# Where side work and block loads stand in the second half of a fused retention and feed-forward kernel

## The chip, the cores and the metric

The kernel runs on one core of a Trainium2 chip. The metric is the device time of one execution in microseconds; the median of three runs of the kernel before is 927.27 us (925.92 to 928.62). The engines have the profile's names: PE is TensorE (PEld its weight loads), DVE VectorE, ACT ScalarE, POOL GpSimd, SP SyncE. SP and ACT both issue transfers here. Each engine works through its own instructions in order, and waits on semaphores of others.

## The reference

```python
# attention: batch 8, heads 8, sequence 576, head dimension 64, fp32
scores = scale * np.matmul(q, k.transpose(0, 1, 3, 2))
gamma = 1.0 - 2.0 ** (-5.0 - np.arange(H, dtype=np.float32))
rel = pos[:, None] - pos[None, :]
Dmat = np.where(rel >= 0, gamma[:, None, None] ** rel[None, :, :], 0.0)
out = np.matmul(scores * Dmat[None], v)
# (B, H, S, D) -> x of (4608, 512), then the feed-forward part; the weights are float64
a = x @ w1            # 512 x 1024
b = x @ w2
h = a * b @ w3        # 1024 x 1024
return (h @ w_out).astype(np.float32)   # 1024 x 512
```

## The kernel before, in words

**Attention in rounds.** The decay is split into a factor for q and one for k and v, so that the retention runs in chunks with a carried state. Batches go in pairs; the sequence is cut into NC = 5 chunks, one of 64 rows and four of 128. There are G = 20 rounds `g`, four pairs by five chunks. A round transposes q and k of the next chunk (`front`, `front_blocks`), scales q and v (`scale_blocks` L184, `scale`, on GpSimd), and multiplies scores (L232), state (L254) and output (L273, L298).

**Loads by blocks.** `load_blocks` (L159) brings q or k of a chunk in pieces of 32 by 32, so that VectorE's block transpose (L189) finishes the transposition. That takes 16 transfers for a full chunk and 8 for the short one, of 32 KB each in runs of 128 bytes; all are issued by SyncE (L170). From round 7 on both q and k come so (`in_blocks`). The tiles of both share a pool tag with two buffers, so that the blocks of a round can come only when those of the round before have been transposed.

**The feed-forward part** multiplies by a form of Strassen's algorithm with seven products. `w3 @ w_out` is multiplied out beforehand. `up` (L506) is one step with one level, for the first tokens. For the later ones `up2` (L959) is one step of a second level: seven products of two matmuls, in PSUM tiles of a pool with seven buffers, of which ScalarE copies the first (L991) and VectorE adds the others (`plus`, L980), each addition on the result of the one before; ScalarE copies the first tile a second time (L1003), GpSimd combines steps (`combine`, L985), VectorE multiplies the two halves (`multiply`, L948). What comes last in a step, the product that goes on in p5's tile and its addition, is left to the next step (`rest`, `finish`). A group has 14 such steps, and then three `down` (L623), each of seven products of four matmuls and their sums and stores.

**The forms of the weights** for the second level are computed once by VectorE (`weight_forms`, L841), stored in HBM (`kept`) and read back, 896 KB a step, into a ring of three (`next_forms`, L899). `open_second` (L883) starts this: it issues the first two loads.

**The order of the work** is written out by hand. The list `todo` holds the items (`up`, `up2`, `down`); `dealt` says how many a round does (1, 1, 2, 2, 2, 3, 4, 4, 4, 3, 7, 7, 3, 7, 7 for rounds 5 to 19), and `work(n)` does n of them. The list `aside` holds side operations: transposes of the next round, and the sums that a `down` needs ahead (`ahead`). In `up2` one is taken after each `plus` (L982), in `down` all that are left ahead of the last addition (L680). `spread` does the same with VectorE's operations on the weights. In the loop of rounds (L1063 to L1118) a round with blocks first scales q of the next chunk (L1076), does all items but one, puts the two transposes into `aside`, does the last item, and then loads the blocks of q and k of the chunk after that.

The program runs through its items in the order written; a transfer also waits for an earlier one that used the same completion semaphore, and the two issuing queues share these.

Of the kernel before, what the change touches and what calls it, by code (L numbers as in the profile page):

```python
# [19 lines left out]
def kernel(  # L20
# [13 lines left out]
    nc = tc.nc  # L34
# [7 lines left out]
    BL = 32  # L42
# [5 lines left out]
    NC = (S + P - 1) // P  # L48
# [107 lines left out]
        live["S", fp] = True  # L156
        yield

    def load_blocks(g, nm):  # L159

        i, c = divmod(g, NC)
        n = sizes[c] // BL
        t = pools["ld"].tile([P, 2 * NP, P // BL, BL], F32, tag="ld_q", name="bl_" + nm)
        src = {"k": k, "q": q}[nm][2 * i:2 * i + 2].rearrange("b (p a) s d -> a (b p) s d", a=2)
        for a in range(2):
            for f in range(D // BL):
                part = (a * (D // BL) + f) * BL
                for m in range(n):
                    s0 = starts[c] + m * BL
                    nc.sync.dma_start(t[part:part + BL, :, m, :],  # L170
                                      src[a, :, s0:s0 + BL, f * BL:(f + 1) * BL].rearrange("m r x -> r m x"))
        live["bl_" + nm, g] = t

    def scale_blocks(g):
# [387 lines left out]


    aside, owed, spread = [], [], []

    def w3_sums():

# [55 lines left out]
    def down(x, y, then=None, last=False):  # L623
        a, done, left = pair_of(x, y)
        ahead(x, y)
        while len(done) < 3:
            aside.pop(0)()
        if then:
            ahead(*then)
        ps = {}  # L630
        ot = pools["ot"].tile([P, 2, 2, DM // 2], F32, tag="ot", name="ot")

        def product(nm, A, B, on=None):
            ps[nm] = ps[on] if on else acc.tile([P, DM // 2], F32, tag="acc", name="po")
            for f in range(NP):
                nc.tensor.matmul(ps[nm], a[A][:, f, :], live["W"][B][:, f, :], start=(f == 0 and not on),  # L636
                                 stop=(f == NP - 1), skip_group_check=True)

        def plus(nm, to, sb):
            nc.vector.tensor_add(ot[:, to[0], to[1]], ps[nm], ot[:, sb[0], sb[1]])  # L640
            if spread:
                spread.pop(0)()

        def put(m, t, row, half=slice(0, 2)):

            i, n = every[m]
            r0 = t * P
            while r0 < (t + 1) * P:
                b = r0 // TB
                e = min((b + 1) * TB, (t + 1) * P)  # L650
                r = (2 * i + b) * S + n * TB + r0 - b * TB
                stores.append((out[r:r + e - r0, half.start * DM // 2:half.stop * DM // 2],
                               ot[r0 - t * P:e - t * P, row, half].rearrange("p h d -> p (h d)")))
                r0 = e
            if not keep_stores:
                store()

        C11, C12, C21, C22 = (0, 0), (0, 1), (1, 0), (1, 1)
        product(1, "A11", "B11")
        first = ot[:, 0, 0]  # L660
        if "first" in live:
            first = live["first"].pop(0)
            live["first"].append(first)
        nc.scalar.copy(first, ps[1])  # L664
        product(7, "S3", "T3")
        product(2, "A12", "B21", on=1)
        nc.vector.tensor_tensor(out=a["S4"], in0=a["A12"], in1=a["S2"], op=ALU.subtract)
        product(6, "S2", "T2")
        nc.vector.tensor_add(ot[:, 0, 1], ps[6], first)
        nc.scalar.copy(ot[:, 0, 0], ps[2])  # L670
        plus(7, C21, C12)
        product(5, "S1", "T1")
        plus(5, C22, C21)
        product(4, "A22", "-T4")
        plus(4, C21, C21)
        put(*y, 1)
        if last:
            put(*x, 0, slice(0, 1))
        product(3, "S4", "B22", on=5)
        while aside:  # L680
            aside.pop(0)()
        plus(3, C12, C12)
        put(*x, 0, slice(1 if last else 0, 2))

    stores, keep_stores = [], []
# [197 lines left out]
    def open_second():  # L883
        while spread:
            spread.pop(0)()
        ra = [wp.tile([P, 32 * P], F32, tag=f"wA{h}", name="ra") for h in halves]
        cs = [wp.tile([P, 2, 4, 2, TB], F32, tag=f"wS{h}", name="cc") for h in halves]
        ring.extend([ra[0][:, :FORM], ra[0][:, FORM:2 * FORM], ra[1][:, :FORM]])
        free.extend(cs[h][:, j] for h in halves for j in range(2))
        live["first"] = [ra[0][:, 2 * FORM + j * DM // 2:2 * FORM + (j + 1) * DM // 2] for j in range(2)]  # L890
        live["T2"] = ra[1][:, FORM:].rearrange("p (s k c t) -> p s k c t", s=2, k=3, c=2)
        live["E"] = ffn.tile([P, 4, 2, TB], F32, tag="c", name="e", bufs=1).rearrange("p (e r) b t -> p e r b t", e=2)
        live["E4"] = pools["carry"].tile([P, KF, P], F32, tag="carry", name="e4").rearrange("p f n -> p (f n)")[
            :, :4 * TB].rearrange("p (r b t) -> p r b t", r=2, b=2)
        for _ in range(2):
            next_forms()
        live["U"] = [ffn.tile([P, 2, TB], F32, tag="T", name="u", bufs=5) for _ in range(5)]

    def next_forms():  # L899
        n = sent[0]  # L900
        if n < 14 * len(groups):
            nm = NAMES.index(OPERANDS[order[n % 7]][0])
            nc.scalar.dma_start(ring[n % 3], kept[n % 14 // 7][nm])
            sent[0] += 1

    def token_forms(gr):
# [52 lines left out]
    def up2(gr, n):  # L959
# [19 lines left out]

        def plus(ps, to, sb):  # L980
            nc.vector.tensor_add(c[:, to], ps, c[:, sb])  # L981
            if aside:  # L982
                aside.pop(0)()

        def combine(part):  # L985
            for into, of in adds:
                o, i = sums2[into][:, part], sums2[of][:, part]
                nc.gpsimd.tensor_tensor(out=o, in0=o, in1=i, op=ALU.add)  # L988
# [3 lines left out]
        p6 = product(None, "S2", "T2")  # L992
        finish()
        next_forms()
        plus(p6, 1, 0)
        plus(product(None, "S3", "T3"), 2, 1)
        p5 = product(None, "S1", "T1")
        plus(p5, 3, 2)
        plus(product(None, "A22", "-T4"), 2, 2)
        combine(slice(2, 4))  # L1000
        multiply()
        product(p1, "A12", "B21")
        nc.scalar.copy(c[:, 0], p1)  # L1003

        def rest():
            product(p5, "S4", "B22")
# [46 lines left out]
    g = NC  # L1053
# [9 lines left out]
    for g in range(NC, G):  # L1063
        c = g % NC
        n = dealt[g - NC]
        if g + 2 < G and not in_blocks[g + 2]:
            load(g + 2, "k")
            load_blocks(g + 2, "q")
        if g + 1 < G:
            scale(g + 1, "v")  # L1070
            if not in_blocks[g + 1]:
                front(g + 1, "k")
                front_blocks(g + 1, "q")
        half = (n + 1) // 2
        if in_blocks[g + 1]:
            scale_blocks(g + 1)  # L1076

            work(n - 1)
            aside.extend(lambda nm=nm: front_blocks(g + 1, nm) for nm in "kq")
            work(1)  # L1080
            while aside:
                aside.pop(0)()
            half = 0
        elif g + 1 == G:
            work(n)
            half = 0
        if in_blocks[g + 2]:
            load_blocks(g + 2, "q")
            load_blocks(g + 2, "k")
        work(half)  # L1090
        pv(g)()

        if g + 2 < G:
            queue = nc.scalar if in_blocks[g + 2] else nc.sync
            load(g + 2, "v", queue)
            if in_blocks[g + 2] and (g + 2) % NC != NC - 1:
                load(g + 2, "k")
        if g + 1 < G:
# [65 lines left out]
```

## Time and profile before

| | |
|---|---|
| time, median of three | 927.27 us |
| span of the profiled run | 920.9 us |
| mean granted clock of TensorE | 0.962 |
| PE, PEld busy | 90%, 81% |
| DVE, POOL, ACT busy | 67%, 41%, 24% |
| moved by transfers | 128.78 MB, 140 GB/s on average |

The chain of work that ended last is by engine: PE 52%, DVE 19%, DMA 12%, SyncE's issuing 7%. In a line of the waits the columns are: who waited, for whom, how long in total, how often, and the longest. In a line of the timeline: start, duration, engine, line, operation, what it writes from what it reads, how many merged, and in brackets how long the engine stood idle before and who released it. Rounds of the second level lie about so in time: round 10 ends near 409 us, 11 near 439, 12 near 476, 13 near 513, 14 near 557, 15 near 596, 16 near 647, 17 near 689, 18 near 729, 19 near 775; then come three `down`, the last 14 steps and the last three `down`.

### The profile page before, as it was taken

How to read it: one execution, taken by the hardware profiler on the slowest of the kernel's cores; microseconds unless marked ns; L12 is line 12 of the kernel's file. 1: busy time of each engine (PE TensorE's matmuls, PEld its weight loads, DVE VectorE, ACT ScalarE, POOL GpSimd, SP SyncE). 2: the span in 40 equal slices, each digit the busy share in tenths (PEclk: the TensorE clock that was granted, in tenths of full speed). 3: DMA queues.
4: the chain of work that ended last, by engine and by line, in shares of the span. 5: the costliest groups of instructions: out<-in, count | busy, mean ns of one | idle time of the engine just before them, and what ended most of it. 6: DMA issues, size and time to landing. Idle time of an engine off the chain costs nothing.

```text
span 920.9 us, 15659 instructions
## 1 busy us (share of the span) xinstructions
PE 831.1 (90%) x6049; PEld 744.5 (81%) x6049; DVE 613.1 (67%) x931; ACT 224.1 (24%) x429; POOL 376.8 (41%) x251
## 2 busy tenths in 40 slices
PE   7999999999999789588696999987999998899988
PEld 6889999447899767488685879977889997798977
DVE  4989999945444776156577745868646878568753
ACT  4786565820211000111111002211011220011200
POOL 1100010011031210566638934858915779537730
PEclk7999999999999999789897999998999999999999
DMA  9994643551364775987585208875428451154401
GB/s 190 219 211 105 117 123 114 154 88 16 74 130 87 193 206 184 243 187 206 138 199 151 46 37 226 224 196 149 88 61 216 160 200 50 37 183 167 154 24 46
DMA packets 247402, 128.78 MB, mean 140 GB/s; under 512 B 202904, under 2 KB 229272, under 8 KB 247328
## 3 DMA queue, kind: packets, MB, share of 16 engines
q1 hardware_dynamic: 203296, 54.86, 29.9%
q10 hardware_dynamic: 44032, 72.92, 24.7%
q8 instruction: 47, 0.77, 0.4%
q14 instruction: 27, 0.22, 0.1%
HBM read 105.46 MB, written 22.28 MB: 139 GB/s over the span
## 4 chain that ended last, share of the span: by engine, by line
PE 52%; DVE 19%; DMA 12%; SPq 7%; issue 5%; POOL 4%; ACT 1%; ACTq 0%; DVEq 0%; POOLq 0%
PE po L636 17%; PE up L976 16%; PE up L523 7%; PE ps L476 6%; SPq L170 5%; DVE cc L981 4%; DVE ab L956 4%; DMA bl_q<-in_q_dram 4%; DMA bl_k<-in_k_dram 3%; DMA kept<-wA 2%; POOL cc L988 2%; PE xps L298 2%; DMA ld_v<-in_v_dram 2%; PE sc L232 2%; DVE c L528 1%
## 5 line engine op out<-in xcount | busy, mean ns | idle before, releaser
L988 POOL TENSOR_TENSOR cc<-cc 128x768 f32<-128x768 f32 x112 | 208.8, 1884 | 86.7 <-DVE cc L981 85.2
L981 DVE TENSOR_TENSOR cc<-up,cc 128x384 f32<-128x384 f32 x280 | 151.3, 552 | 60.4 <-PE up L976 41.6
L636 PE MATMUL po<-w3o,ab 128*128 128x256 f32 x552 | 129.3, 389 | 24.1 <-ACT ra L664 18.6
L636 PEld LDWEIGHTS po<-w3o,ab 128*128 128x128 f32 x552 | 105.8, 194 | 42.4 <-ACT ra L664 20.2
L976 PE MATMUL up<-xT,ra 128*128 128x192 f32 x512 | 107.3, 341 | 31.1 <-DVE cc L981 18.4
L976 PEld LDWEIGHTS up<-xT,ra 128*128 128x128 f32 x512 | 88.2, 196 | 36.6 <-DVE cc L981 22.1
L203 POOL TENSOR_TENSOR ld_v<-ld_v,gk 128x1024 f32<-128x1024 f32 (+1 forms) x18 | 34.4, 1911 | 174.1 <-DMA ld_v<-in_v_dram 172.1
L956 DVE TENSOR_TENSOR ab<-cc 128x384 f32<-128x384 f32 x64 | 82.8, 1334 | 32.7 <-POOL cc L988 32.7
L180 POOL TENSOR_TENSOR bl_q<-bl_q,gqs 128x512 f32<-128x512 f32 (+1 forms) x30 | 30.5, 1038 | 119.1 <-DMA bl_q<-in_q_dram 93.9
L976 PE MATMUL up<-ra 128*128 128x192 f32 x384 | 77.8, 333 | 0.7 <-DMA ra<-kept 0.6
L1003 ACT COPY cc<-up 128x384 f32<-128x384 f32 x56 | 26.8, 479 | 206.1 <-PE up L976 138.2
L976 PE MATMUL up<-e,ra 128*128 128x192 f32 x384 | 73.4, 327 | 1.1 <-DVE cc L981 0.9
L523 PE MATMUL up<-xT,wA 128*128 128x192 f32 x384 | 70.7, 328 | 0.3 <-DVE xT L495 0.3
L528 DVE TENSOR_TENSOR c<-up,c 128x384 f32<-128x384 f32 x80 | 44.0, 549 | 36.6 <-PE up L523 36.0
L976 PEld LDWEIGHTS up<-ra 128*128 128x128 f32 x384 | 66.0, 194 | 1.5 <-PE up L976 1.2
L636 PE MATMUL po<-wB,forms 128*128 128x256 f32 x288 | 65.3, 380 | 2.0 <-DVE forms L609 2.0
L976 PEld LDWEIGHTS up<-e,ra 128*128 128x128 f32 x384 | 64.3, 191 | 1.7 <-DVE cc L981 1.2
L523 PEld LDWEIGHTS up<-xT,wA 128*128 128x128 f32 x384 | 63.3, 190 | 1.7 <-PE up L523 0.6
L636 PEld LDWEIGHTS po<-wB,forms 128*128 128x128 f32 x288 | 54.6, 190 | 10.1 <-issue 1.9
L976 PE MATMUL up<-u,ra 128*128 128x192 f32 x288 | 56.3, 333 | 5.7 <-DVE cc L981 5.7
L235 DVE TENSOR_TENSOR pm<-sc,mask 128x512 f32<-128x512 f32 (+1 forms) x80 | 45.4, 626 | 23.4 <-PE sc L232 23.4
L640 DVE TENSOR_TENSOR ot<-po,ot 128x256 f32<-128x256 f32 x72 | 30.4, 422 | 38.4 <-PE po L636 37.6
(106 smaller groups left out, 1235.4 us busy)
## 6 DMA issues: line engine op xcount, KB each, us to landing
ra<-kept ACTq DMA_DIRECT2D x56, 896.0 KB, 4.7
raw<-in_moe_w_dram SPq DMA_DIRECT2D x72, 128.0 KB, 3.0
bl_q<-in_q_dram SPq DMA_DIRECT2D x216, 32.0 KB, 3.2
ld_k<-in_k_dram SPq DMA_DIRECT2D x13, 512.0 KB, 6.0
bl_k<-in_k_dram SPq DMA_DIRECT2D x192, 32.0 KB, 2.4
kept<-wA SPq DMA_DIRECT2D x24, 256.0 KB, 3.3
out_dram<-ot ACTq DMA_DIRECT2D x23, 256.0 KB, 2.0
ld_v<-in_v_dram ACTq DMA_DIRECT2D x11, 512.0 KB, 5.7
```

Source lines behind the costliest of these rows:

```text
L170: nc.sync.dma_start(t[part:part + BL, :, m, :], src[a, :, s0:s0 + BL, f * BL:(f + 1) * BL].rearrange("m r x -> r m x"))
L180: nc.gpsimd.tensor_tensor(out=part, in0=part, in1=gqs[:, :, n0:n0 + n].unsqueeze(3).to_broadcast([P, NP, n, BL]), op=ALU.mult)
L203: engine.tensor_tensor(out=t, in0=t, in1=gam[:sz, c].unsqueeze(1).unsqueeze(3).to_broadcast([sz, 2, H, D]), op=ALU.mult)
L235: nc.vector.tensor_mul(pm[:sz, b, j, :, :sz], sc[j][:sz, :, :sz], mask[:sz, :sz].unsqueeze(1).to_broadcast([sz, NP, sz]))
L476: nc.tensor.matmul(ps, live["w3T", ft][:, g, :], live["wo"][:, g, :], start=(g == 0), stop=(g == KF - 1))
L523: nc.tensor.matmul(ps[:, w, :], a[:, w, r, :], b[:, r, :], start=(new and w == r == 0), stop=(w == r == 1), skip_group_check=True)
L528: nc.vector.tensor_add(c[:, to], ps, c[:, sb])
L636: nc.tensor.matmul(ps[nm], a[A][:, f, :], live["W"][B][:, f, :], start=(f == 0 and not on), stop=(f == NP - 1), skip_group_check=True)
L956: nc.vector.tensor_mul(ab, v[:, :, 0, :], v[:, :, 1, :])
L976: nc.tensor.matmul(ps[:, w, :], weight_of(slot, a, w), B[b], start=(new and w == 0), stop=True, skip_group_check=True)
L981: nc.vector.tensor_add(c[:, to], ps, c[:, sb])
L988: nc.gpsimd.tensor_tensor(out=o, in0=o, in1=i, op=ALU.add)
```

## The change

Five edits, which all move work and take none away:

1. q of the next chunk is scaled ahead of the last two items of a round and not ahead of all. It is meant to keep GpSimd from waiting for blocks with the combinations queued behind.
2. From round 10 on the blocks of k are put in a list `small`, which ScalarE issues: four after the first form load of a step and four after its second copy, or at two places of a `down`; what is left goes ahead of the scaling.
3. An `up2` step takes one side operation, after its four first additions, in place of one after each addition.
4. From round 10 on a `down` takes a side operation after each addition but the last, and what is left after the last addition in place of ahead of it.
5. The first two form loads are issued by SyncE, and the second sums of the weights start one slot of `spread` later.

```diff
+    small = []
+
+    def issue(n):
+        for _ in range(min(n, len(small))):
+            small.pop(0)()
+
-    def load_blocks(g, nm):
+    def load_blocks(g, nm, later=False):
...
-                    nc.sync.dma_start(t[part:part + BL, :, m, :],
-                                      src[a, :, s0:s0 + BL, f * BL:(f + 1) * BL].rearrange("m r x -> r m x"))
+                    to = t[part:part + BL, :, m, :]
+                    of = src[a, :, s0:s0 + BL, f * BL:(f + 1) * BL].rearrange("m r x -> r m x")
+                    if later:
+                        small.append(lambda to=to, of=of: nc.scalar.dma_start(to, of))
+                    else:
+                        nc.sync.dma_start(to, of)
...
# in down
             nc.vector.tensor_add(ot[:, to[0], to[1]], ps[nm], ot[:, sb[0], sb[1]])
             if spread:
                 spread.pop(0)()
+            if g >= 2 * NC and aside and nm != 3:
+                aside.pop(0)()
...
         nc.scalar.copy(first, ps[1])
+        issue(4)
         product(7, "S3", "T3")
...
         nc.scalar.copy(ot[:, 0, 0], ps[2])
+        issue(4)
         plus(7, C21, C12)
...
         product(3, "S4", "B22", on=5)
+        while aside and g < 2 * NC:
+            aside.pop(0)()
+        plus(3, C12, C12)
         while aside:
             aside.pop(0)()
-        plus(3, C12, C12)
...
# in open_second
         for _ in range(2):
-            next_forms()
+            next_forms(nc.sync)
...
# in up2
         def plus(ps, to, sb):
             nc.vector.tensor_add(c[:, to], ps, c[:, sb])
-            if aside:
-                aside.pop(0)()
...
         finish()
         next_forms()
+        issue(4)
...
         combine(slice(2, 4))
+        if aside:
+            aside.pop(0)()
         multiply()
         product(p1, "A12", "B21")
         nc.scalar.copy(c[:, 0], p1)
+        issue(4)
...
# in the loop of rounds
         if in_blocks[g + 1]:
+            work(n - 2)
+            issue(len(small))
             scale_blocks(g + 1)
-
-            work(n - 1)
             aside.extend(lambda nm=nm: front_blocks(g + 1, nm) for nm in "kq")
-            work(1)
+            work(2)
             while aside:
                 aside.pop(0)()
...
             load_blocks(g + 2, "q")
-            load_blocks(g + 2, "k")
+            load_blocks(g + 2, "k", later=g >= 2 * NC)
...
-            forms = [(lambda h=h, second=second: spread.extend([lambda: None] * second + weight_forms(h, second)),)
+            forms = [(lambda h=h, second=second: spread.extend([lambda: None] * (2 * second) + weight_forms(h, second)),)
                      for h in halves for second in (False, True)]
```

More of the change, by code (lines that the diff above doesn't have):

```diff
@@ L564 @@
     aside, owed, spread = [], [], []
+    g = 0
     def w3_sums():
@@ L895, in open_second, with next_forms @@
         for _ in range(2):
-            next_forms()
+            next_forms(nc.sync)
         live["U"] = [ffn.tile([P, 2, TB], F32, tag="T", name="u", bufs=5) for _ in range(5)]
-    def next_forms():
+    def next_forms(engine=nc.scalar):
         n = sent[0]
@@ L902, in next_forms @@
             nm = NAMES.index(OPERANDS[order[n % 7]][0])
-            nc.scalar.dma_start(ring[n % 3], kept[n % 14 // 7][nm])
+            engine.dma_start(ring[n % 3], kept[n % 14 // 7][nm])
             sent[0] += 1
```

## The prediction

> **What bounds the kernel now.** I read the page's shares and slices first, then the table by stretches, then the waits, then the timeline round each stretch in which TensorE stands still.
>
> ```profile
> PE 831.1 (90%) x6049; PEld 744.5 (81%) x6049; DVE 613.1 (67%) x931; ACT 224.1 (24%) x429; POOL 376.8 (41%) x251
> PEclk7999999999999999789897999998999999999999
> 440.00:475.00 35.00, 24.66 (x219) 23.36 (x219) 21.71 (x30) 5.39 (x11) 17.38 (x11) 0.90 0.67 165
> 475.00:510.00 35.00, 25.97 (x188) 24.28 (x188) 23.68 (x32) 3.83 (x8) 23.66 (x14) 0.81 0.59 147
> 600.00:640.00 40.00, 30.89 (x186) 29.48 (x188) 28.79 (x43) 5.26 (x12) 27.88 (x16) 0.91 0.63 178
> ```
>
> The columns of the last three are busy PE, PEld, DVE, ACT, POOL, then clock, DMA share and GB/s. TensorE is the bound on the whole, but between 300 and 690 us it loses up to ten of 35 us to idle time, and its granted clock falls to 0.81. Nothing else is full there: those stretches wait in chains.
>
> ```profile
> POOL bl_q L180 <- DMA bl_q<-in_q_dram: 93.9, 3, 80.5
> POOL bl_q L180 <- DMA bl_k<-in_k_dram: 21.9, 5, 5.4
> DVE ab L956 <- POOL cc L988: 32.7, 11, 8.5
> ACT xT L305 <- DMA kept<-wA: 21.0, 1, 21.0
> SPq L170 <- DMA ra<-kept: 31.1, 13, 6.6
> ```
>
> GpSimd waits in L180 for the blocks of q, and VectorE's multiplications (L956) wait for GpSimd's combinations (L988), which are queued behind it. Round 12 shows the chain whole:
>
> ```profile
> 445.17 16.51 SPq L170 DMA_DIRECT2D bl_k<-in_k_dram  x16
> 449.74 2.06 POOL L180 TENSOR_TENSOR bl_q<-bl_q,gqs 128x512 f32<-128x512 f32 x2 [5.40 <-DMA bl_k<-in_k_dram]
> 453.60 4.22 DVE L956 TENSOR_TENSOR ab<-cc 128x384 f32<-128x384 f32 x2 [8.51 <-POOL cc L988]
> 455.89 2.93 PE L976 MATMUL up<-xT,ra 128*128 128x192 f32 x8 [7.70 <-ACT cc L991]
> ```
>
> The other kinds of hole are VectorE's transposes and sums between two additions (504.75, 637.40), the same ahead of the last addition of a down (531.48), and ScalarE caught in the first form loads (380.68):
>
> ```profile
> 371.41 4.48 ACTq L903 DMA_DIRECT2D ra<-kept  x2
> 380.68 3.49 PE L636 MATMUL po<-w3o,ab 128*128 128x256 f32 x8 [11.19 <-ACT ra L664]
> 504.75 1.65 PE L976 MATMUL up<-xT,ra 128*128 128x192 f32 x4 [5.09 <-DVE cc L981]
> 531.48 1.99 PE L636 MATMUL po<-w3o,ab 128*128 128x256 f32 x8 [2.69 <-ACT ra L664]
> 637.40 1.65 PE L976 MATMUL up<-xT,ra 128*128 128x192 f32 x4 [4.72 <-DVE cc L981]
> L170 SPq DMA_DIRECT2D bl_q<-in_q_dram x216: 311/449/2487, 193.2 to 695.7; - x108
> ```
>
> **What the Trainium skill says.** "TensorE: Matmul & The Clock Gate", section "What's actually happening", has the clock halved after about 3.4 us of idleness. The trace agrees: after the holes of 5.09 and 4.72 us four records take 1.65 us, otherwise 0.81. A long hole so costs some 2.7 us more. "DMA: Bandwidth & Descriptors", section "Issuing engines are not separate DMA queues", says that a second issuing engine saves only issue time, as all transfers share 16 engines. Here an issue is 0.449 us on SyncE's queue, and 16 blocks take 8 to 16.5 us. "SBUF — State Buffer", section "SBUF: two separate sides", has VectorE and GpSimd lock one port pair against each other. The trace agrees: the sum of L605 takes 0.68 us alone and up to 2.24 us beside GpSimd.
>
> **The change, part by part.** A second-level step has 28 matmul records, four per 0.65 us: 4.55 us. State, values and scores add 1.03 + 1.90 + 0.93 + 1.99 = 5.85 us to a round (433.70 to 439.5). The floor of a round is 24.05 us with four steps and 37.7 us with seven.
>
> 1. *Scaling ahead of the last two items, k off SyncE's queue, transposes one per step.* Rounds 11, 12, 13 and 16 took 30.5 (409.0 to 439.5), 36.8 (to 476.3), 36.75 (to 513.05) and 50.8 us (596.05 to 646.87): 6.4 + 12.7 + 12.7 + 13.1 = 44.9 us over their floors, holes and cold clock together. Rounds 15 and 18 (38.1 and 40.2 us) have nothing much to give. With the scaling two steps later q's blocks have had about 15 us to land (12 us of issue and 3 us of flight) and GpSimd no longer stands in front of the combinations. VectorE does per step five additions of 0.55 us and 8/7 multiplications of 1.33 us: 4.27 us. With 2.5 us of transposes and 2.5 us of masking that is 22.1 of 24.05 us in a four-step round, so little slack is left, and I don't count on the floor: 75%, 34 us. Bounds: half (22 us), 90% (40 us).
>
> 2. *k's 16 blocks on ScalarE, in fours.* No row shows block issues on this queue. From below: 0.449 us each with 0.04 between, 7.9 us per round of 16. From above: about 1 us each, SyncE's slowest round (16.5 us for 16). Eight go into each of two steps, on top of two copies of 0.48 us and a form load of 0.33 us. Laid out over the 4.55 us step: the form load goes at 2.0 us, as it waits for the ring, the first four issues end by 4.3 us (cheap) or 5.2 us (one slowed by the form load ahead of it), the copy of L1003 follows, four more end at 7.0 to 7.7 us, and only then does the next step's first copy (L991) run, which was ready at 5.2 us. In the second step the delay grows to between 2.5 and 4 us. Queued behind it are L1003, which frees a PSUM bank that the third product of the next step takes, L991, on which all of VectorE's additions of that step hang, and the next form load, which has about 2.4 us to spare (4.7 us to land). With cheap issues all just fits, 0.5 us; with dear ones TensorE waits some 5 us. I take 2.3 us in each of the six rounds with steps (11, 12, 13, 15, 16, 18): 14 us; bounds 3 and 30. The waits between transfers raise the upper end: blocks on SyncE already waited 31.1 us for form loads to land, so a block on ScalarE may wait likewise, with the copies behind it.
>
> 3. *The flush of what is left ahead of the scaling.* In round 17 only one down precedes it, so eight issues, about 4 us, stand ahead of L664 of the second down. That copy releases the bank of the third product, 3.5 us after the down's start. I take 2.5 us (0 to 5).
>
> 4. *Side operations in a down.* After the last addition, and spread over the earlier ones, the sums no longer hold back the store and the copy that TensorE waits for: 2.69 + 1.63 + 3.05 (at 788.36) = 7.4 us. Against it, in round 14 the transpose of q now sits in the second down, at about 534 us, while GpSimd has q scaled only at 538 us, behind the token sums. I take 5 us (3 to 7).
>
> 5. *First forms by SyncE.* ScalarE's copy comes some 5 to 9 us sooner and most of the hole at 380 us closes. But the next stage hangs on SyncE: blocks of q from 373.31 us, of k from 386.23 to 394.5 us, transposed at 400.11 us, and scores at 405.26 us. The two loads now stand ahead of these blocks and wait for the stores of the weights, and the transpose of k moves one step forward. TensorE, early, then waits for k. The gain is given back: I take a loss of 1 us (gain 3 to loss 4). The extra empty slot in `spread` moves VectorE's weight sums past one addition, away from a wait for stores (the hole of 4.01 us at 321 us), and sends the last forms about 2 us later; it ends in the same wait, at nothing.
>
> Sum: 34 + 5 - 14 - 2.5 - 1 = 21.5 us; 927.3 - 21.5 = **906 us**.
>
> **The rivals.**
> - *Everything fits* (cheap issues, 90% of the excess, all three holes of the downs, flush and forms free): 40 + 7 - 3 = 44 us, **883 us**. For it: ScalarE is busy 24%, and two steps have room for 10.5 us of its work in 9.1 us, nearly enough. Against it: VectorE's thin slack and round 17.
> - *The transfers are the bound anyway*: k by another queue lands no sooner, as the DMA engines are 0.6 to 0.75 busy in these stretches, and the transpose, one step earlier, waits. Only 35% of the excess comes back: 16 + 5 - 14 - 2.5 - 1 = 3.5 us, **924 us**. For it: SyncE takes up to 16.5 us for 16 blocks, far above 16 times 0.449. Against it: q and k went one after the other before and now overlap.
> - *ScalarE becomes the bound*, and the kernel slower: 60% of the excess and 4 us of the downs (31 us), against 30 us of stalls, 5 of flush and 4 of forms: 8 us slower, **935 us**. For it: every addition of a step hangs on a copy of this queue, which issues and waits in order. Against it: it idles most of a step today.
>
> **How the numbers follow.** The forecast has 0.57, everything fits 0.15, transfers 0.12, ScalarE 0.16. Predicted is the forecast's 906 us. The range runs from 886 us, near the best case, to 930 us, past the transfers' case; outside lie most of the slower case and the tail of the best. Faster by over 0.3% (under 924.5 us): 0.57 + 0.15 + 0.07 of the transfers' case = 0.79; within 0.3%: 0.05; slower: 0.16.
>
> **What would show it.** Right: the waits of L180 for blocks shrink to a few us in rounds 11 to 13 and 16, no hole of TensorE there is above 3 us, and the clock stays above 0.95; L956 waits under 15 us for GpSimd; the holes at the downs are gone. ScalarE's copies L991 and L1003 start late in the first two steps of a round, with short holes of TensorE behind them. The hole at 380 us is smaller and one ahead of the scores near 400 us is larger. Wrong: form loads that TensorE waits for, or a ScalarE queue standing on another transfer for over 5 us, would mean the slower case; a transpose of k that waits for its blocks for several us in each round, the transfers' case.

## The result and the profile after

The changed kernel takes **937.72 us** (median of three, 936.82 to 942.21) against 927.27: a ratio of 1.0128 with the 95% interval [1.0085, 1.0171]. Run again on another chip it came to 1.0069 [1.0034, 1.0105]. It is slower by 6 to 12 us. The forecast was 906 us, range 886 to 930, with 0.16 for slower.

The engines' busy time, and TensorE's busy tenths and granted clock over 40 slices, of the kernel after (its profiled run is the one of 942.21 us, with a span of 939.5 us and a mean clock of 0.953; a slice is 23.5 us):

```profile
PE 843.4 (90%) x6049; PEld 754.1 (80%) x6049; DVE 613.6 (65%) x931; ACT 224.1 (24%) x429; POOL 378.9 (40%) x251
PE   8899999999995997758797999978899998999988
PEclk7999999999997998989998999898999999999999
```

The work of VectorE, ScalarE and GpSimd is the same to within about 2 us. TensorE is busy 12.3 us longer with as many instructions, that is at a lower clock, and idle 6.3 us longer. Its row has a 5 in the 13th slice (282 to 305 us), and the clock a 7, where the kernel before has nines (its slice from 276 to 299 us); later the clock stays below nine tenths in five slices between 352 and 658 us, as many as before.

Two of the stretches that the prediction showed, in the kernel after (columns as there: busy PE, PEld, DVE, ACT, POOL, then clock, DMA share, GB/s):

```profile
440.00:475.00 35.00, 27.84 (x247) 26.66 (x246) 25.20 (x35) 6.44 (x13) 23.80 (x15) 0.90 0.87 196
600.00:640.00 40.00, 33.65 (x235) 32.23 (x232) 26.25 (x43) 6.40 (x14) 22.53 (x14) 0.92 0.67 173
```

TensorE does get more done in them (27.84 and 33.65 us busy against 24.66 and 30.89; 31.01 against 25.97 in the third, 475 to 510 us). So the edit works where it was aimed. The waits say the same, and show what came in its place (who waited, for whom, total, times, longest):

```profile
DVE kT L199 <- DMA bl_k<-in_k_dram: 23.4, 2, 11.8
PE up L993 <- ACT cc L1006: 20.7, 14, 5.1
ACT cc L1006 <- DMA bl_k<-in_k_dram: 20.1, 5, 5.9
PE up L533 <- DVE c L538: 14.3, 4, 10.6
ACT ra L677 <- DMA bl_k<-in_k_dram: 13.3, 1, 13.3
DVE ab L973 <- POOL cc L1003: 12.2, 8, 3.0
```

GpSimd's scaling (L190, before L180) waits 2.6 us for blocks of the round in place of 21.9, and VectorE's multiplications (L973, before L956) wait 12.2 us for GpSimd in place of 32.7. In their place there are three new waits: ScalarE's copies in the steps (L1006, before L991) and in a `down` (L677, before L664) stand behind block issues, and VectorE stands at a transpose of k for 11.8 us, which becomes 10.6 us of TensorE in the first-level step `up` (L533).

**Where the time went.** I cut both traces at the ends of the scores of each round, worked out from the timelines (us; the differences are of the unrounded times):

| rounds | before | after | after - before |
|---|---|---|---|
| 7 | 25.5 | 37.7 | +12.2 |
| 8, 9, 10 | 110.2 | 113.4 | +3.2 |
| 11, 12, 13, 14 | 148.4 | 137.4 | -10.9 |
| 15, 16, 17, 18 | 171.8 | 184.1 | +12.3 |

Round 19, the last steps and the last `down`s add nothing (-0.1 us); about 2 us of the spans' difference lie ahead of all this, in the start. A table like this compares one execution with one other: the spans differ by 18.6 us, the medians by 10.4, and a second trace of the changed kernel (after_again below) has 36.8, 112.3, 134.7 and 182.0 us in these four rows. So differences of 2 to 3 us in a row say little, while those of 10 us and more stand. One round that the prediction doesn't mention loses more than rounds 11 to 14 gain.

Round 7 in the kernel before, in the timeline (start, duration, engine, line, operation, and the idle time before with its releaser):

```profile
288.11 1.25 DVE L189 STREAM_TRANSPOSE kT<-bl_k 128x1024 f32<-128x1024 f32 x1 [2.22 <-DMA bl_k<-in_k_dram]
291.44 1.57 PE L523 MATMUL up<-xT,wS 128*128 128x192 f32 x8 [1.02 <-DVE c L528]
```

and in the kernel after:

```profile
290.52 1.25 DVE L199 STREAM_TRANSPOSE kT<-bl_k 128x1024 f32<-128x1024 f32 x1 [11.79 <-DMA bl_k<-in_k_dram]
293.85 2.93 PE L533 MATMUL up<-xT,wS 128*128 128x192 f32 x8 [10.59 <-DVE c L538]
```

The blocks of k land at about the same point of the round in both, some 15 us after the scores of the round before (273.3 and 275.3 us). Round 7 has two items. Before, the transposes came in the second of them, so VectorE had the additions of the first to do and waited 2.22 us. Now `work(n - 2)` does nothing there, the transposes sit behind the first additions of the first `up`, and VectorE stands still for 11.79 us with all later additions behind it; TensorE runs out of PSUM tiles and comes back cold (2.93 us for eight matmuls, warm 1.57).

Rounds 12, 16 and 17 of the kernel after show the second new wait (ACTq is ScalarE's queue issuing transfers):

```profile
462.72 5.29 ACTq L179 DMA_DIRECT2D bl_k<-in_k_dram  x4
468.11 0.48 ACT L1006 COPY cc<-up 128x384 f32<-128x384 f32 x1 [4.94 <-DMA bl_k<-in_k_dram]
468.64 2.93 PE L993 MATMUL up<-xT,ra 128*128 128x192 f32 x8 [5.08 <-ACT cc L1006]
...
608.64 0.33 ACTq L920 DMA_DIRECT2D ra<-kept  x1
...
616.16 1.83 ACTq L179 DMA_DIRECT2D bl_k<-in_k_dram  x4
618.03 0.48 ACT L1006 COPY cc<-up 128x384 f32<-128x384 f32 x1 [5.91 <-DMA bl_k<-in_k_dram]
618.56 0.92 PE L993 MATMUL up<-xT,ra 128*128 128x192 f32 x4 [3.46 <-ACT cc L1006]
...
677.75 0.37 ACT L677 COPY ra<-po 128x256 f32<-128x256 f32 x1 [13.27 <-DMA bl_k<-in_k_dram]
678.17 3.65 PE L647 MATMUL po<-w3o,ab 128*128 128x256 f32 x8 [3.89 <-ACT ra L677]
```

Four issues take 1.83 us when they follow each other, and 5.29 us when one of them has to stand. What it stands for can be read in the trace: the issue waits on its own completion semaphore, which an earlier form load used. In round 12 the load issued at 459.66 us lands at 467.67 us, and the last of the four blocks goes at 467.69 us. In round 16 the load of 608.64 us lands at 616.14 us, and the queue, free since 612.1 us, stands for 4.0 us ahead of the first of its four blocks, at 616.16 us. Over the whole trace ScalarE's queue stands 19.8 us for form loads, its own ones. The copy that opens the next step follows the last issue within 0.1 us, and TensorE follows the copy: it waits 5.08 us in round 12 and 3.46 us in round 16. In round 17 it is the flush, and there no issue stands: eight in a row take 4.00 us, with the copy of the second `down` behind them, for which TensorE waits 3.89 us. (The 13.27 us in front of that copy are idle time of ScalarE's arithmetic, not of its queue.)

### The profile page after: what moved, and what is told of

The parts are those of the page before. It is cut to its first block, busy times and chain, and to the rows that moved or that the text cites. A ratio compares the mean times of both kernels' runs of the same rounds, so it can differ in the third digit from the quotient of the medians.

```text
span 939.5 us, 15664 instructions
## 1 busy us (share of the span) xinstructions
PE 843.4 (90%) x6049; PEld 754.1 (80%) x6049; DVE 613.6 (65%) x931; ACT 224.1 (24%) x429; POOL 378.9 (40%) x251
## 4 chain that ended last, share of the span: by engine, by line
PE 55%; DVE 17%; DMA 12%; POOL 4%; issue 4%; SPq 4%; ACT 2%; ACTq 1%; POOLq 0%; DVEq 0%
PE po L647 19%; PE up L993 13%; PE up L533 11%; DVE ab L973 6%; PE ps L486 6%; DVE cc L998 5%; DMA ra<-kept 4%; PE sc L242 2%; PE xps L308 2%; DMA ld_v<-in_v_dram 2%; POOL cc L1003 2%; SPq L181 2%; DMA bl_k<-in_k_dram 2%; DMA bl_q<-in_q_dram 1%; ACTq L179 1%
## 5 line engine op out<-in xcount | busy, mean ns | idle before, releaser
L998 DVE TENSOR_TENSOR cc<-up,cc 128x384 f32<-128x384 f32 x280 | 152.1, 555 | 79.4 <-PE up L993 36.4
L647 PEld LDWEIGHTS po<-w3o,ab 128*128 128x128 f32 x552 | 105.6, 194 | 29.8 <-ACT ra L677 10.1
L973 DVE TENSOR_TENSOR ab<-cc 128x384 f32<-128x384 f32 x64 | 88.9, 1430 | 12.3 <-POOL cc L1003 12.2
L647 PE MATMUL po<-wB,forms 128*128 128x256 f32 x288 | 69.6, 398 | 6.8 <-DVE forms L620 6.8
L533 PE MATMUL up<-xT,wA 128*128 128x192 f32 x384 | 72.1, 333 | 0.0
L538 DVE TENSOR_TENSOR c<-up,c 128x384 f32<-128x384 f32 x80 | 44.1, 551 | 42.1 <-PE up L533 41.5
L993 PEld LDWEIGHTS up<-ra 128*128 128x128 f32 x384 | 64.1, 190 | 9.1 <-ACT cc L1006 9.0
L647 PEld LDWEIGHTS po<-wB,forms 128*128 128x128 f32 x288 | 57.7, 201 | 16.5 <-DVE forms L620 4.0
L190 POOL TENSOR_TENSOR bl_q<-bl_q,gqs 128x512 f32<-128x512 f32 (+1 forms) x30 | 31.0, 1054 | 92.3 <-DMA bl_q<-in_q_dram 89.7
L533 PEld LDWEIGHTS up<-xT,wA 128*128 128x128 f32 x384 | 65.1, 194 | 1.1 <-issue 0.5
L681 DVE TENSOR_TENSOR ab<-ab,forms 128x512 f32<-128x512 f32 x17 | 17.9, 1056 | 58.2 <-PE po L647 58.2
L486 PE MATMUL ps<-wo,w3T 128*128 128x512 f32 x128 | 55.1, 592 | 0.0
```

The source lines that it names most:

```text
L190: nc.gpsimd.tensor_tensor(out=part, in0=part, in1=gqs[:, :, n0:n0 + n].unsqueeze(3).to_broadcast([P, NP, n, BL]), op=ALU.mult)
L486: nc.tensor.matmul(ps, live["w3T", ft][:, g, :], live["wo"][:, g, :], start=(g == 0), stop=(g == KF - 1))
L533: nc.tensor.matmul(ps[:, w, :], a[:, w, r, :], b[:, r, :], start=(new and w == r == 0), stop=(w == r == 1), skip_group_check=True)
L973: nc.vector.tensor_mul(ab, v[:, :, 0, :], v[:, :, 1, :])
L993: nc.tensor.matmul(ps[:, w, :], weight_of(slot, a, w), B[b], start=(new and w == 0), stop=True, skip_group_check=True)
```

## The experiments

My theory after this: (a) round 7 alone costs 11 to 12 us and has nothing to do with the aim of the change; (b) ScalarE's issues cost some 14 us, as forecast; (c) the scaling later in the round is a gain, but below the 34 us forecast. The rivals: the loss is all ScalarE's; or the early order is a loss everywhere and round 7 only its largest part; or the first forms by SyncE upset rounds 9 and 10. The twelve kernels were run in three groups. A ratio is to the kernel before, on the same chip, whose medians were 928.10, 928.81 and 931.68 us. All kernels start from the changed one.

**late10: the order of before up to round 10, all else as changed.** First group, with the next three.

```diff
+            early = g > 2 * NC
+            if early:
-            work(n - 2)
-            issue(len(small))
+                work(n - 2)
+                issue(len(small))
             scale_blocks(g + 1)
+            if not early:
+                work(n - 1)
+                issue(len(small))
             aside.extend(lambda nm=nm: front_blocks(g + 1, nm) for nm in "kq")
-            work(2)
+            work(2 if early else 1)
```

> The changed kernel, but up to round 10 with the order of before: scaling ahead of all items, all items but one, then both transposes in the last item. Theory A (the transposes, moved one item forward, meet blocks of k that SyncE has not yet brought: hole of 10.6 us in round 7, of 8.5 us in round 10): some 12 us come back, about 925 us, near the kernel before. Theory B (ScalarE's issuing of blocks costs the time): at most 3 us come back, 934 us or more.

Measured: 923.44 us, 0.994 [0.9909, 0.9971]. Against the changed kernel's 1.0069 to 1.0128 this gives back 1.3 to 1.9% of 928 us, 12 to 17 us. Round 7 takes 25.0 us again.

```profile
286.78 1.25 DVE L199 STREAM_TRANSPOSE kT<-bl_k 128x1024 f32<-128x1024 f32 x1 [1.69 <-DMA bl_k<-in_k_dram]
```

This line of late10 stands for the one with 11.79 us above: the blocks land as before, VectorE waits 1.69 us, and TensorE afterwards 0.49 us. Theory (a) holds. The other rounds that this run puts back, 8 to 10, take 114.0 us against 113.4, so the time comes from round 7.

**ksync: all blocks of k by SyncE, all else as changed.**

```diff
-            load_blocks(g + 2, "k", later=g >= 2 * NC)
+            load_blocks(g + 2, "k")
```

> The changed kernel, but all blocks of k issued by SyncE, none by ScalarE. Theory A: nothing comes back, 937 to 945 us, as the gain of rounds 11 to 13 shrinks. Theory B: the holes of TensorE behind ScalarE's copies go (20.7 us of waits in the trace), 922 to 928 us.

Measured: 921.55 us, 0.9899 [0.9852, 0.9947]. Round 7 stays long (36.4 us), while rounds 15 to 18 fall from 184.1 to 168.2 us. Against the changed kernel's ratios this gives back 16 to 21 us.

**late10_ksync: both.**

> Both of the first two together: order of before up to round 10, and all blocks of k by SyncE. Theory A alone: as the first of these, about 925 us or a few us above. Theory B alone: as the second, 922 to 928 us. Both hold and add: 910 to 918 us, faster than the kernel before.

Measured: 911.67 us, 0.9788 [0.9742, 0.9834]. Against late10 the step is 1.5% of 928 us, 14 us, by the medians 11.8; against ksync it is 10 us. The waits of this kernel, beside those of after:

```profile
DVE kT L199 <- DMA bl_k<-in_k_dram: 22.5, 5, 7.7
PE up L993 <- ACT cc L1006: 5.3, 6, 2.9
```

TensorE's wait for ScalarE's copies falls from 20.7 us (17.2 in late10) to 5.3. VectorE still waits little for GpSimd (10.1 us), so this gain did not need k on another queue. What ScalarE's issues did buy is seen best in round 11 of late10_ksync:

```profile
434.65 1.25 DVE L199 STREAM_TRANSPOSE kT<-bl_k 128x1024 f32<-128x1024 f32 x1 [6.95 <-DMA bl_k<-in_k_dram]
436.39 1.19 PE L283 MATMUL xps<-qT,sb 64*64 64x128 f32 x28 [4.23 <-DVE cc L998]
```

With SyncE bringing both, k comes late and TensorE loses 4.23 us (round 11: 30.5 us against 27.8 in late10). In round 13 k's transpose waits once more, 4.02 us; VectorE's multiplication and ScalarE's next copy stand behind it, and TensorE waits 2.88 us, which is part of the 5.3 us above. So two of the suspects add up: the order up to round 10 and ScalarE's issues together are worth more than the whole loss, and the rest of the change is a gain of 2.1% (16 us by the medians, 20 by the ratio).

**fscal: the first two form loads by ScalarE again.**

```diff
-            next_forms(nc.sync)
+            next_forms()
```

> The changed kernel, but the first two form loads issued by ScalarE as before. Theories A and B: within 4 us of the changed kernel, 934 to 942 us. Theory C (the loads ahead of the blocks on SyncE's queue delay rounds 9 and 10): 6 us or more come back, 931 us or less.

Measured: 930.55 us, 1.0028 [0.9999, 1.0056], 4 to 9 us below the changed kernel. The blocks behind the first form loads (which SyncE issues at 386.84 us), in the kernel after:

```profile
388.29 15.03 SPq L181 DMA_DIRECT2D bl_q<-in_q_dram  x16
388.37 3.49 PE L647 MATMUL po<-w3o,ab 128*128 128x256 f32 x8 [5.17 <-ACT ra L677]
403.42 12.64 SPq L181 DMA_DIRECT2D bl_k<-in_k_dram  x16
419.69 1.76 PE L308 MATMUL xps<-pm,ld_v 64*64 64x64 f32 x28 [8.46 <-DVE cc L998]
```

and in fscal:

```profile
380.82 13.07 SPq L181 DMA_DIRECT2D bl_q<-in_q_dram  x16
388.32 3.78 PE L647 MATMUL po<-w3o,ab 128*128 128x256 f32 x8 [11.30 <-ACT ra L677]
393.99 9.11 SPq L181 DMA_DIRECT2D bl_k<-in_k_dram  x16
410.68 1.03 PE L308 MATMUL xps<-pm,ld_v 64*64 64x64 f32 x28 [2.83 <-DVE cc L998]
```

With the loads on ScalarE the hole at 380 us is whole (11.30 us) and the later one small (2.83); with SyncE they are 5.17 and 8.46. The sums are 14.1 and 13.6 us: the hole is moved. Round 10 is all the same 3.9 us longer with the loads on SyncE (47.8 us against 43.9). On SyncE the blocks wait behind the two loads and are also slower to issue (27.7 us for 32, against 22.2).

**l10_ks_fs: late10_ksync and fscal in one.** Second group, with the next three.

> The kernel with the order of before up to round 10 and all blocks of k by SyncE, and the first two form loads by ScalarE again. Theory C (the loads ahead of the blocks on SyncE's queue delay round 10, which took 49.8 us with them and 44.9 us before): some 5 us come back, about 907 us. Rival (the delay has another cause): within 2 us of the version without this edit, 911 us.

Measured: 911.73 us, 0.9832 [0.9782, 0.9881]. That is not below late10_ksync's 0.9788, so the forms by SyncE cost something measurable only beside ScalarE's issues, if at all. The intervals overlap, and are too wide to show or exclude the 5 us of theory C here.

**l10_ks_fs_s1: the same with the weight sums at the old place of `spread`.**

```diff
-            ... spread.extend([lambda: None] * (2 * second) + weight_forms(h, second)) ...
+            ... spread.extend([lambda: None] * second + weight_forms(h, second)) ...
```

> The same, and the second sums of the weights one slot of the spread list earlier, as before. Rounds 8 and 9 together take 65.3 us before and 64.4 us in the version with the order of before up to round 10, so the slot is expected to be worth nothing: within 2 us of the kernel without this edit. Rival (the later slot sends the last forms late and costs round 9 what it gives to round 8): 3 us or more faster.

Measured: 910.73 us, 0.9817 [0.9779, 0.9855], no difference that the intervals could show. Round 8 goes from 24.4 to 29.7 us and round 9 from 41.4 to 34.6: the slot moves the waits from one round into the other (TensorE's longest one is 3.65 us in round 8 with the early slot, 9.40 us in round 9 with the late one).

**no_down: l10_ks_fs with `down` as before the change.**

```diff
-            if g >= 2 * NC and aside and nm != 3:
-                aside.pop(0)()
...
-        while aside and g < 2 * NC:
-            aside.pop(0)()
-        plus(3, C12, C12)
         while aside:
             aside.pop(0)()
+        plus(3, C12, C12)
```

> The order of before up to round 10, k by SyncE, first forms by ScalarE, and the downs as before, with all side operations ahead of the last addition. The prediction's 5 us for the edit in the downs: some 5 us slower than with that edit, holes of 2 to 3 us at the downs back. Rival (the edit is worth nothing, as in the rounds after 19 the changed kernel gained nothing): within 2 us.

Measured: 912.15 us, 0.9837 [0.9794, 0.988], against 911.73: no gain of the edit of `down` is seen. Each interval is about 4 us wide to either side, so the run does not exclude the 5 us either. The traces show a part given back: no_down has holes of 1.83, 1.82 and 1.92 us (rounds 14, 17 and after 19) ahead of the matmuls that wait for a copy, which l10_ks_fs lacks, while the holes ahead of the first matmuls of a `down`, which wait for a sum of VectorE (L616), add up to 5.7 us in rounds 14 and 17 of l10_ks_fs and to 2.6 in no_down.

A second loss at the `down`s is in both of these kernels, so it does not explain their equal times, but it explains why the last part of the kernel after gains nothing. The hole of 3.05 us of before at 788.36 us is gone there, but the first `down` of each last three now starts late. The last such start of the kernel after:

```profile
902.99 5.41 PE L647 MATMUL po<-wB,forms 128*128 128x256 f32 x16 [3.56 <-DVE forms L620]
```

where before has

```profile
886.04 3.72 PE L636 MATMUL po<-wB,forms 128*128 128x256 f32 x16 [0.46 <-DVE forms L609]
```

(The other pair is 3.26 us, then 5.38, against 1.50 and 3.69.) The sums that a `down` needs are side operations of the last step ahead of it. Edit 3 moves them from behind the first addition to behind the fourth, next to the multiplications, so they come 2 to 3 us later, and the 16 matmuls run at a lower clock, for a further 1.7 us.

**l10_twos: late10 with `issue(2)` in all four places.** Half the dose, to see whether the loss goes with the number of issues in front of a copy or with the queue as such.

> The order of before up to round 10, ScalarE issuing the blocks of k, but two and not four at each place. If ScalarE loses by more issue time than two steps hold, half the dose over twice the steps fits: rounds 16 and 18 come down from 51 and 40 us to about 46 and 39, 916 us or less. If it loses by waits on earlier transfers, whatever the dose, the time stays at 920 to 925 us.

Measured: 917.92 us, 0.9902 [0.9866, 0.9937], between late10 (0.994) and late10_ksync (0.9788). TensorE's wait for L1006 falls from 17.2 to 9.1 us, and rounds 16 and 18 reach 44.1 and 38.9 us, all that k by SyncE gives there. The time lies between the two expectations, and the dose is not cleanly halved: what the steps no longer take falls to the flush. In rounds 11 to 13 ten blocks go in one row (4.8 to 6.4 us), and in round 17 twelve:

```profile
651.47 6.00 ACTq L179 DMA_DIRECT2D bl_k<-in_k_dram  x12
657.93 3.78 PE L647 MATMUL po<-w3o,ab 128*128 128x256 f32 x8 [5.88 <-ACT ra L677]
```

Twelve issues stand before the copy, TensorE waits 5.88 us where after has 3.89, and round 17 takes 51.5 us against 48.1 in late10 (round 14: 47.4 against 43.8). With twos the queue also stands less for form loads (5.3 us in all, 14.4 in late10), so this run does not tell the two causes apart.

**l10_twos_d4: twos in the steps, fours in a `down`.** Third group, with the last three.

> The order of before up to round 10, ScalarE issuing the blocks of k, two at each place of a step and four at each place of a down. With twos everywhere round 17 took 51.5 us, as twelve blocks were left to flush. If ScalarE's loss is issue time in front of copies, round 17 comes back to 48 us and rounds 16 and 18 stay at 44 to 46 and 39 us: 912 to 916 us. If not, 918 us or more.

Measured: 916.28 us, 0.9855 [0.9815, 0.9896], between the two expectations again. The flush in round 17 is eight issues again and its hole 3.88 us, as in after. But the rounds hardly follow: 50.4 us for round 17, and 47.0 for round 14, where the flush's hole is gone and one ahead of the first matmuls of the `down`, which waits for a sum of VectorE (L616), grew from 1.71 to 3.28 us. I can't say where the other 2 us of round 17 went; its trace is of the execution of 921.51 us, and the median is 916.28.

**after_again: the changed kernel once more**, to have it on the chip of the others.

> The changed kernel itself, beside the versions made from it and on the same chip: 1.01 to 1.015 of the kernel before, as measured first.

Measured: 937.17 us, 1.0069 [1.0034, 1.0105], a little less than expected; the interval reaches 1.01.

**late9: as late10, but the order of before only up to round 9.** It asks whether the hole of 8.46 us in round 10 comes from the early transposes as well.

```diff
-            early = g > 2 * NC
+            early = g > 2 * NC - 1
```

> The order of before only up to round 9; round 10 as in the changed kernel. If the hole of 8.5 us in round 10 comes from the transposes one item early, it stays here and goes in the version with the order of before up to round 10: some 5 us slower than that one, 928 us. If it comes from the first form loads on SyncE's queue, both are alike, 921 to 925 us, and round 7 alone explains what the order of before brings.

Measured: 925.21 us, 0.9942 [0.9922, 0.9962], the same as late10. Its hole in round 10 is 8.91 us, ahead of the product with v (L308); late10 has one of 9.36 us just behind that, ahead of the state (L264), which ends in a wait for the load of k's rows. The hole is there with either order, and small with the forms on ScalarE (fscal 2.83 us, best 2.89). So it belongs to edit 5. Of the rounds whose order both kernels undo, only round 7 gets shorter by it (8 to 10 together: 113.4 in after, 114.0 in late10). The rival that the early order loses everywhere falls with this, and with rounds 11 to 13, which keep it in late10_ksync and are 12 us below before; the rival that ScalarE loses everything fell with late10, which leaves ScalarE's issues as they are.

**best: late9 and k by SyncE and forms by ScalarE, and the first sum of a `down` behind the first addition of the last step.** The sum goes into a list of its own, `soon`:

```diff
         def plus(ps, to, sb):
             nc.vector.tensor_add(c[:, to], ps, c[:, sb])
+            if soon:
+                soon.pop(0)()
...
-            ahead(*nxt[1:], 1 if fn is up2 else 3)
+            ahead(*nxt[1:], 1 if fn is up2 else 3, soon if fn is up2 else None)
```

> What the runs point to: order of before up to round 9, all blocks of k by SyncE, first forms by ScalarE, side operations one per step from round 10 on, but the first sum of the next down after the first addition of the last step, as before. Theory (the end of each group loses as this sum waits behind the multiplications; tail of 114 us against 111.5): 2 us better than the other versions without ScalarE's issuing, 908 us or less. Rival (the sum's place is worth nothing): 910 to 913 us.

Measured: **909.79 us, 0.9776 [0.9745, 0.9808]**, faster than both kernels, but above the 908 us of the theory and just below the rival's 910. The starts of the last `down`s are those of before again, here the last:

```profile
874.79 3.72 PE L647 MATMUL po<-wB,forms 128*128 128x256 f32 x16 [0.45 <-DVE forms L620]
```

The three `down`s after round 19 take 38.3 us in place of 41.6 before, and the last three 42.0 in place of 47.2 in late10_ksync (before 42.3). In the ratios that is 0.56 points to l10_ks_fs (5 us) and 0.12 to late10_ksync (1 us); the intervals overlap, so the worth of the sum's place is not shown. The kernel still has round 11's hole for k's blocks (4.72 us).

Rounds in groups, for the kernels that the argument uses (us, from the timelines):

| rounds | before | after | late10 | ksync | late10_ksync | best |
|---|---|---|---|---|---|---|
| 7 | 25.5 | 37.7 | 25.0 | 36.4 | 25.3 | 26.3 |
| 8 to 10 | 110.2 | 113.4 | 114.0 | 112.8 | 114.5 | 112.0 |
| 11 to 14 | 148.4 | 137.4 | 135.2 | 136.7 | 136.2 | 136.2 |
| 15 to 18 | 171.8 | 184.1 | 181.6 | 168.2 | 170.3 | 171.6 |

## Why the prediction was wrong

The sum failed in its first term: step 1 took the cost of the new order outside the rounds it was aimed at as nothing, without a reason, and so left out round 7; and it counted too much gain. The total of the costs of ScalarE's issues and of the flush was sized well. Between 906 us and what was measured lie 28 to 32 us: some 12 are round 7, and some 18 a gain of steps 1, 4 and 5 of 20 us in place of 38. Gains have a plus here, losses a minus.

1. **Scaling ahead of the last two items (forecast: +34 us). This step failed, in two ways.** It counted the excess of rounds 11 to 13 and 16 and took for granted that the new order costs nothing elsewhere. But the loop runs from the first round with blocks on, and in round 7, with two items, it puts the transposes ahead of blocks that land 15 us into the round. This lost 12.2 us in the trace and 12 to 17 us in the ratios of late10. The information was in the trace of before: VectorE's transpose of round 7 already waited for these blocks, by 2.22 us, in the second item, so in any earlier place the transpose could only wait longer. Step 5 does reckon with this move of the transpose, but for round 10 alone. The step also mis-sized the gain. late10_ksync, which has neither round 7's loss nor ScalarE's issues, is 2.1% below before, 20 us [15, 24] for steps 1, 4 and 5 together (16 by the medians), where the forecast had 34 + 5 - 1 = 38. By rounds: 11 to 13 fall from 104.0 to 92.0 us and 16 from 53.5 to 45.4, which is 20 us of the 34. (The forecast had 50.8 us for round 16 and 38.1 for round 15, as it let round 15 end at 596.05 us; its scores end at 593.34.) Of the 20 us round 15, which was said to have nothing much to give, takes 4.7 back (35.9 to 40.7), and rounds 8 to 10 another 4.3. The spans of these two traces differ by 8.2 us only, less than ratio and medians say, so the split by rounds is rough. In round 15 q's transpose comes in the last step (585.20 us), directly ahead of the scores:

```profile
586.49 3.78 PE L242 MATMUL sc<-qT,kT 64*128 64x128 f32 x32 [0.79 <-DVE qT L199]
```

This line is late10_ksync's; the 32 matmuls of the scores take 3.78 us, before 2.06: the granted clock is 0.51 from 586 to 591 us. The Trainium skill's page "TensorE: Matmul & The Clock Gate", section "What's actually happening", has the half clock after some 3.4 us of idleness; here the holes ahead of the scores are 0.56, 0.80 and 0.79 us, within some six us, so the page's figure does not account for it, and what lowered the clock stays open. That one side operation per step trades the holes between additions for some at the end of a round is read from this trace; no run takes edit 3 alone back. The forecast counted the first and not the second.

2. **k's blocks on ScalarE (forecast: -14 us, bounds 3 and 30).** Right in mechanism and in the total: late10 to late10_ksync is 12 (medians) to 14 us (ratios), after to ksync 16 to 21, with the flush in both; the two terms together were 16.5. That the total fits is in part luck. The forecast spread 2.3 us over each of six rounds; between the traces of late10 and late10_ksync 5.8 of the 11.3 us of rounds 15 to 18 lie in round 16 alone, and rounds 11 to 14 cost nothing together (135.2 and 136.2 us), as k from SyncE comes late in round 11. The issue itself was the cheap one of the two bounds, 0.46 us in the median of 120. The Trainium skill's page "DMA: Bandwidth & Descriptors", section "Issuing engines are not separate DMA queues", calls the time to start a transfer "usually small relative to the DMA itself"; it is, 0.46 us of the 4.0 us to landing. The dear part are the waits for earlier transfers, which the forecast had put into the upper end (four issues in 5.29 us, 19.8 us of standing for form loads in all), and the copies that queue behind them. The edit bought little for it: from round 11 on late10_ksync has two holes of TensorE that follow from k's late landing, 4.23 us in round 11 and 2.88 in round 13.

3. **The flush in round 17 (forecast: -2.5, bounds 0 and 5).** The hole is 3.89 us, within the bounds. The round takes 48.4 us, in late10_ksync 45.3, but in l10_ks_fs, which has no flush either, 48.1; so what the hole costs the round is not settled.

4. **Side operations in a `down` (forecast: +5).** Not seen: 0.4 us by the medians of no_down and l10_ks_fs, with intervals that would still allow the 5. The holes went as the step says, and a part of them came back ahead of the first matmuls of a `down`. The step also did not look at where edit 3 takes the sums of the next `down`, which starts 1.8 to 3.1 us later; in the trace of best, where the first sum is back in its place, these starts are those of before.

5. **First forms by SyncE (forecast: -1, gain 3 to loss 4).** Right in the trace: the hole at 380 us fell from 11.19 to 5.17 us, and where before has two of 1.30 and 1.77 us ahead of the state and the scores there is one of 8.46, because the blocks stand behind the two loads. In the ratios the changed kernel loses 4 to 9 us by it, at or beyond the forecast's worse end of 4; in late10_ksync no loss is seen. Of the slot in `spread` no effect is seen either, as the step said.

6. **The rivals and the range.** The nearest was ScalarE as the bound, 935 us. It came near the number, but not by its own path, and that is luck: its sign ("a ScalarE queue standing on another transfer for over 5 us") did not come, as the longest stand in the trace is 4.0 us, and ScalarE's share of the loss was about the forecast's own; what took the kernel past before was round 7, which no rival had. Of the forecast's signs, L180 and L956 waiting less came true (2.6 and 12.2 us), as did the holes at 380 and 400 us; no hole above 3 us and a clock above 0.95 did not (5.08 and 3.46 us in rounds 12 and 16, clock 0.90 and 0.92 in the stretches shown). The transfers' case, with transposes that wait for k in each round, holds for rounds 7 and 10 and not for the later ones. The parts close the sum: 20 us below before for late10_ksync, plus 14 for ScalarE and 12.2 for round 7 in the trace, make 6 us above it, the 1.0069 of after_again. That they close so well is chance, as each is known to some 4 us only and 12.2 comes from one pair of traces. The range of 886 to 930 us took in the bounds of each listed step but had no place for an unlisted one.

**What stays open:** the sizes below 5 us (edit 5, the first sum in best) are not resolved by the intervals, and neither is round 17 of l10_twos_d4. How the gain of 20 us divides between the later scaling (edit 1) and one side operation per step (edit 3) was not tested: every run keeps both from round 11 on. Whether k on ScalarE for round 11 alone, where it saves the hole of 4.72 us, beats best was not tried.

## What to carry to other kernels

An edit of a loop acts on each round it runs in: list all rounds with their item counts, not those the edit is aimed at, and for each moved operation compare its new place with the moment at which its data land. A queue that also issues transfers passes on every wait of an issue to the compute instructions behind it; before moving issues there, ask who waits for the next copy, and whether the queue they came from had in fact been late. When two operations of one engine change places, the one that moved back needs a price as well as the one that moved ahead.

## What the runs showed of the hardware

- A block issue takes as long on ScalarE's queue as on SyncE's when nothing is in the way (0.46 us, before 0.449). Four took between 1.83 and 5.29 us, because an issue stood until an earlier transfer on its completion semaphore had landed. ScalarE's queue stood up to 4.0 us at a time, 19.8 us in all for its own form loads, and its copies stood with it.
- After two loads of 896 KB on SyncE's queue, 32 issues of blocks took 27.7 us; with these loads on ScalarE, 22.2.
- A hole of 3.3 to 3.9 us ahead of 16 matmuls of 256 columns made them take 5.3 to 6.8 us in after, after_again and late10_ksync (after_again has 6.71 us after the same hole of 3.3 us for which after has 5.38); after holes of 0.5 and 1.5 us they took 3.7.
- The granted clock also fell to 0.51 without a long hole: in late10_ksync after three of 0.56, 0.80 and 0.79 us ahead of the scores of round 15.
